# Unit 2 of a two-layer transformer kernel gets its Strassen projection, and attention's products move into the weights' slots

## The chip, the cores and the metric

The kernel runs on one core of one Trainium2 chip. A core has a matrix engine (TensorE, called PE in the profile, with its weight loads in a row of their own, PEld), a vector engine (VectorE, DVE), a scalar engine with table functions (ScalarE, ACT), a general engine (GpSimd, POOL) and a queue engine (SyncE, SP) that issues nearly all DMA transfers here. They run side by side and wait for each other by semaphores. SBUF is the memory on the chip in which all tiles lie; PSUM is the small memory of 8 banks into which TensorE writes. The metric is the device time of one execution, in microseconds; the time given for a kernel is the median of several runs.

## The reference: what is computed

The input is one sequence of 2048 tokens with 1024 channels in bf16. Two layers follow, and both use the same weights. Each layer is attention on the normalised input, added to the input, and then a feed-forward part on the normalised result, added again:

```python
x = x + _A_ref(_layernorm(x, axis=-1), A_wqkv, A_wo)
x = x + _B_ref(_layernorm(x, axis=-1), B_w1, B_b1, B_w2, B_b2)
```

`_A_ref` projects to q, k and v (1024 to 3 x 1024, 32 heads of 32 channels). A token attends to 8 tokens: itself and those 2, 4, ... 14 places before it. It takes the products of q with the 8 keys, a softmax over these 8 (places before the start are masked), and the weighted sum of the 8 values, and projects with `wo`. `_B_ref` is `h = x @ w1 + b1` (3584 wide), `relu(h)` squared, and `h @ w2 + b2`.

## The kernel before

**Units.** As the steps of the window are two tokens wide, even and odd tokens never meet in attention. The kernel takes the even tokens first and then the odd ones, so that a window is 8 neighbours in a row. A block is 512 such tokens (`BLK`), a layer has four blocks, and the two layers make 8 units, numbered 0 to 7. The units are staged so that the projections and the attention of unit u+1 stand beside the feed-forward part of unit u.

**Stages of one unit.** `SA` loads the tokens and normalises them (ScalarE) and transposes the result into `xnA`, with channels on the partitions. `SQ` or `SQ7` projects q, k and v. `S2` does attention, nearly all of it on VectorE, in two halves of 256 tokens: `prod` multiplies q with the eight shifted keys (tiles `P`) and adds pairs of them, TensorE sums over the channels of a head (`lg`), ScalarE takes the exponential, `norm` divides (`pb`), and `av` multiplies with the shifted values (tiles `pr`, 128 x 2 x 8 x 256, two channel groups in one tile) and adds the eight up into `o`. `SW` projects `o` with `wo` (PSUM tiles `py`), adds the residual (`xm`), normalises again and gives `xnB`. `SF1` computes the hidden layer into `r2`, and `SF2` multiplies it with `w2` and adds the residual (`xo`).

**Plain and Strassen forms.** A product of matrices cut into 2 x 2 blocks takes 8 block products, or 7 by Strassen's scheme in Winograd's form, at the price of sums and differences of the blocks of both operands and of the results. The weights are the same in both layers and in all units, so their combinations are made once on VectorE (tiles `tv`) and stored to DRAM by DMA, and later units load them. Unit 0 has plain forms in the feed-forward part (`SF1_plain`, `SF2_plain`), and while the weights are there it makes the combinations of `w1` (`keep_w1`, stored in `w1s`) and of `w2` (`keep_w2`, stored in `tw`). The units after it use seven products.

For q, k and v the constant `KEEPQ` says in which unit the combinations are made. Before, it is 2: units 0, 1 and 2 project plainly with `SQ` (line 729: 8 matmuls of 512 columns for each of 24 chunks of 128 channels), and `keep_wq` (line 771) makes the 24 combinations during unit 2's projection, each followed by a store to `wqsk` or `wqsqv`. From unit 3 on `SQ7` does it (line 851). It combines the blocks of the input on VectorE (`TA`, line 550: eight instructions). There are two steps for each of q, k, v, and a step takes 7 products of 8 matmuls of 256 columns in three PSUM banks X, Y, Z. Three times in a step the partial sum in X is copied out (`u`, line 837, ScalarE, or 838, VectorE), three times VectorE adds such a copy to another bank (line 842), and one result is copied out alone (829 or 830). That is 7 evictions where the plain form has 4 (lines 741 and 743) for the same outputs.

**Slots.** Each tile belongs to a class of slots of one size and takes a slot until its last reader is done. `8K` (9 slots of 8192 bytes a partition) holds the weight tiles `w`, the transposed inputs, `TA`, `T`, `o` and `s1`. `8P` (2 slots) holds nothing but `pr`. `2K` (8 slots) holds the combinations `tv` until their store has landed, the token tiles `xt` and `xn`, and the hidden layer's partial sums `rr`. Tags have caps besides: at most 6 `w`, 4 `tv`, 2 `pr`.

**The order of the work.** All operations are recorded first. Then the function `schedule` of class `Plan` orders them by a list scheduler that has a cost for each operation, a model of the DMA queue and the slots, and for every operation a priority and an engine pick (evictions and a few others can go to ScalarE or VectorE). The priorities and picks come from a packed table, `STARTS`, one entry for each operation. The order so found is what each engine gets; an engine executes its queue in that order and waits where an operand or a slot isn't free.

```python
def schedule(self):
    raw = zlib.decompress(base64.b85decode(STARTS))
    n = len(raw) // 3
    assert n == len(self.ops)
    for i, o in enumerate(self.ops):
        o.num, o.prio, o.pick = i, raw[i] + 256 * raw[n + i], raw[2 * n + i]
```

Of the kernel before, what the change touches and what calls it, by code (L numbers as in the profile page):

```python
# [12 lines left out]
F16 = mybir.dt.float16  # L13
# [4 lines left out]
H = 32  # L18
# [16 lines left out]
F_SW, F_H, F_QS, F_AV, F_ORD = 0, 1, 0, 1, 0  # L35
# [12 lines left out]
def _win_ap(a2d, col0, n, nw=W, wstep=-1):  # L48
# [5 lines left out]
    "c-rlG1zgu#(l>vlL%O?50qGP35fJG=DM(2w0us^)(p}PxlyrB8bR!4|2#O*GHY)0S&QI^|z5CqHvv=Qj_uczEpZ)&N%$b=pGiPT0iDH!Fo{3+f{Gji$$;4;YeQ@%F{GDS8ag(i6+Xu%uq%<%2^kJYK"  # L54
    "=8~Tr_7<&J`#0^CG59=K*qD`>Qs7QHPrwmw)KNfOt@hD`&R_mx0TwBjSi1c<XGEXSn*6lzT#etlhB2R*Zz6drW>{94260^polEEJ-Li|Sa>5Ts^?DZQ@LAq(pegyjKRc;Li#l@ud`xO(%R}^VO2O5D"
    "SQ2~wJdDWL0|{{!0!k-Y4t@6!JlEaY3t4a4*p5ze%6UE)k0aOD8#2h_h}mYeBX_)?f6{k8^HG8cw;^MbVLdv)rJ3I`x6CMaok_Qg)xIorYHd-}J)iXsDVKkeQpvvF3+>ZIZw=0tr+udJ{a}=L<PITE"
    "bk29R%FILWH5ajS7@yJ#Wrm3~yip(8v{KG{Jr#6rj8r82)`ebE2*3N*o@2OzR-{_kyY2DWP=m|2+k-p3HYL2L?|TMOq)6I(6n{N#dyD3V5m}#8@Ekgor-?w|>6Mij!OwiyVjOz8Q@U>|QhmAA9%z*Y"
    "ILvWkUSK@`kmS3dVc3_}-bIlHnoB%Z$98b}-%Pz^Y<+SMTc>H?CErr$1<6tdpXKUsS6j;#sas)UAGcjuwr6y>>%9eudy(%=Le5nOROd`|>@_~>IF!@XdH0?mqoXAxZC~c%{IS=PBpMoinMTDkyQ42d"
    "2IxI(CQ6x<1K&GiJXR^IKX-eL>WG9)mq#OExzvkV<*%~7FYCw{u|{}LJ5p-KN{uOG4S!F#D2F+I$Nd?@cAdwJFNRT?<vjnu3{U356Nk4O5=jP|RR>~1jjzwo5&N(D#QQkP_mZc7I^Fh~6Rqy!n$P~J"
    "_!jrxz+st_fZ2xE*T-zP*6z+w-O$xFxi^2U;HWUGj(;URwmwHiz_*2tCzWfO0Z!S`9b-)>Eu(V2@7$I8p-KH;`03PG#E$z{>kC%%Eg6K>KRo1@v>$K2DQR~<c>t46ZN)w<?D&O9{g4}OMHd{>&GKHc"  # L60
    "9FvoB7>J-)7O*0irZTv>@GRQ6bA{db>lp!`aq-ttSayxnL@(Q2jXJ`1kJwmFm*7be%Bp#XH5V@w-s{~jnj_rK7ok}@ryBo+{L--&3H(00YHZ>7@vd}-eP-K|Jy}(%_8!VJ(c=edJAEXPwxiYs{k*i|"
    "Lw59m<es#u@!eD^>OK+n%eWu8L~_nD3Xl6SiLmZ@9Cg+lk-V01Wj<ba(l8ufx^iugPTkir1K;Zfm&!4oOeV|6;j_GMYnr+>B=l2vwd@+qTY_9_Ur}akGlYK8N%jj%%x>Jc`!T6q-cN6#ui}Hv@keEk"
    "xy*TajrN<Z@KrDq+SVMM291kEx1}9@8!cMSzvL$O?ON~*pX(jB()XUCzdj#VeCX59VO`j&Wt+^MvnG0KCbYX)rR<Y>s_b*LEl1zZ0lrfP`zu}QNjz$u@B=Ny=0Pcuj6TX;jvj*ejh2)p*NrOn?q@v3"
    "SBjeUPe*yNJeCN|(rBj%wQZFO{95{C4qqpmQ$Ul)mT1*XFS_}2hBb!rod{ymMOKlMm7*~&od%uU?_(L3gC_WMA2AtWDHQD;M%-m4dir(@hgiv*B#bokYO|k^HIu{Yd(S?!=c6W!h4b=n*xGlMmcMVO"
    "Q3&|l#o;p@>MJA7N;hJCE8~Posa&!+cQ2|@tCc}LV+13MG|jB+9@cY)!qS%lCLzpq2ihsvUA`-HD(MwXhh8^kqayA-Il$4s>?Uw7nAy<#-N*5x`O7<I9`8&wLZ;Y^GfO#5xgARiX4TdmFkX8ROr5kS"
    "eL_KaPp_v^%ApolG&EKyC+t1P<%(rq3z43+2UM|>WY(=!+Tn+~0(?ixx4ujG)-Mp^>BnvbwHleP6k$c*+&6MN;aN>2-DoN9v0=6od5Etk+pqH^?XzL=ns=Q5-Aw=C5{bQ#Lm9@UPI8Sfx@(V|zu>SR"
    "kgbbm&hu9=R%3g}M?SnzoLqW{L&`vIvX9H$OzJ>XsLuMhQnOe1ol*etmwS%=gdKiIB7)T>QeSeIHGQv^_2{Vz5dMT~5$`3rj-i%vY%ldi5RF5HZ^>cUtk9VW<5#^4M7Gpx{twg(G27qlG0y8>>f*UE"
    "xgl1&S<XdX@z_`;4p;YR`FrkM8-WP(=7c525F=*3CP(6L-#t&(iiSR%-ZaK~E3%4fuKTtjigbgl_2Ihd2%ZJDQTP=ZQ7@(o#Z6zrmv^5KDoHp8#aLBlo^F-;(80e=-{P{=Lmc}#DtvHiUwZkdtnf4L"
    "kZY;BiCaS~=C!X47P`}HYBT*uC9mAmecne;QGsjm@q}s16Lxj;IK?OzoD)TPocE7*>YeA)dS<;7RD&hPq~V_{W<EjljP|sv`{(S6Q;~ufHT)g;T<bolaGXy*s+vJ0;PINrG}M75p_2$*^IYzzCu_;s"
    "*eA^7mt8P|776*S&&IiqcNpXkRX!rdF&zu<Ss}w!xb*HEUC5K=D^zAV4=PyeDFqVYJKjirQ%NK><3Q4;nF_lp>cu?WwY>evhvHXb2ixpOrCg7lwanNS>go7g9>1xhaH*s9m26QL(JtHGg3?Yeg^B$8"  # L70
    "R7a(xvDjM=IGuXlC`Qs&4xCdq(CYfA8Qw?Z@>HSTlJtc;Rp>x*ZQbdCRqws5Dl}bxg(GG3mSDJG#QH9?{GnDVtxy|AEc!?zA>HG7#%d4Qp38y<!jTV|iuqF&ymLvf%-Spo`p4a!B2+VCK9l{?zN-6)"
    "cXpI=-pc})w)c1Lq2!LIq)$_G30xmM;MP8njMY1;G>KKX#^Gie>NBxUR{YqENRg`u_sggb+Fz?tx6^N4bH*uv*L9GA^IO5>C(g3SFW0Lp6m&1406T8qyN4qf{%VVC<$kbXa@FoV`@rHz%%FioNs|mZ"
    "17iXX$4TtBlAnSVQ?!!V2{(NDzZVZ2+3CPae`x0wX;!c$MJn}<U(SwqSdZc=lT{Tt(*a2msc63b)(B^{nRWfm=g+1j;^&mzH>dgOY!s4JjlC=n>kjxfQe{?2yt&>+^?&>>*fnH|E<J@W&119|JQ?gP"
    "tLcvt(w7WeI-1C!I7_OJ<FzjlzrbnRhS7!6Jz^2;TBoF4pJLB%y-3u!bB0uvR@<;1LnSq;AE)Du|CUugp>6E)4hMf6=ePAl(b^5JfQowYruJ|ylxpi^cawysZXx#$C6~U9L22qO$2!TB$GEBzyTlPG"
    "a?&>Jq-w4F+mo60d78;%L}ydK$n#U2cO>tld2Ym{obFUjr#m_9?NZC}#!o5hQsueS(SYDHdmnL3QudVm7Os?Rh`W?~PAOFNQn9RmIH8PzgP%TYWxY0CNlDmJNJ40Rb=t<iWCwTHNw=1U*oD#XUW?Fj"
    "p2Zwr#=cAyJ8hk)`-Etz!O&I4P`ZBpn=8Vfl(Hywv&Jc_vb(c(xN@rB4a-cjYo;DlGjm<@*Pdb2Oex{=i{9r7xIwP}#m|Z~cRuE^MA@$LosSQ6R&itv!XkZM6k`RWt93%EzD<61PvCWbN-?>~@x?0)"
    "*TuG^{`1rQiwTQ%Ix%Y5<%{?PTb9d>gyJJ25)@>f&lLn(m;<&9`sCueF{y6Y*R0woe3e!Wp$ORTpruaT<w?$dv4gryuX3yKs#jn4x1xZm?ya3(ULT9T!9Hrb`<(u1CzrD8Ke*&x?|eq7d?EV7p0gfK"
    "EzLv_$EsM6zje)NvWf>hAKYWGM863rem;9YvFG;ur4*N=nK+sxZ&-utc3;nv%d?rgckmmPJBSrOW_M33xKb$*fgfA5h?)Dg)+u+H*fQhBgYf!ij~T@e3GApvFE5yO`aNom#Z{oL>Be|T{07h5x=A#7"
    "#j^ckz11K=K3(x+j=JF;we7Qc-@wm`WU1_gH+?K+i(Dl3vhGP^l+PV0)a9?+<?V{^-`X)$w2)BiJ>`Tu;FU$5K9gXY{gO^O;WdAN3(c@TI|I7XCI>TFxI2oJ+kWuUz*ltaFq3D=#<&}skGJh}Zv4v+"
    "H5G5ZJK@xDobpOn$?ox+8pQ{mN*al!`?x*R8#cvR`_*QdR=k{k6(2eagq`gLS9EfHzCU5BO|eS4u>1T>&{|Qn+ly^V>FI9`SljgPsO+C>%FTC>%yX7#7y6#s{kn6uY>g{#Zza0_1KY-k=v6!e^YSzk"  # L80
    "iOn~WgqrKCURE}Y*fM#<u@6U@4?{ZG9(6uRm=(No(x&Yxd10HP^sWM1yovD#f7Sb5n8ls%HNv>|E;w`eep1wqn#wL}&n$VZP@g@EXFeKt)+|rh&yhT$ckWRm#ck*Q4efrv*U}1<CWpe;B5zNyprf;E"
    "r-fP0++M(><a%qK_(9a4_r}M1qtCHRwQhqdddk&WpOtxy<gdPDSxsEq=jln%!!~f!Ex>1W#SVFqV=GCabfZR;ewzAg{nS^d?CL!6PtT4HzDw%E8s)LS^@VNkT*niWWQq$}n07m;f=>;Ye2<dn>#n8T"
    "+*nh)QTfQt`^z$M@mi3kJ7>3MSS{B@2BR6A(hbAm#mL3DM;?L1sLPoT?d!ir%?s$9XH8i^*_;YyT=qDXLnIyT7fLOVT=q)EeTeJ=uf?jou<7%Y4vr7drP$#c4bPZZy&4iDde*7rLt6!V**=9mZJ^Ld"
    "xb<GfYnH>F&v(pTtDc$x{hGIe&8+PCBiZ|S)Fri*k7bJ<sqED3DpbGJWiDP9!>6#|(-aT1^L{0G`9|sy=V2y~=mP28UGJEdAa#WX;<Wz4%G%9OBi2uCyE!t|aX$*Z@u<H)q|A8Lx4WCtwnT+2;Mq{%"
    "`%Y}LnX_p`hG}dGPvx6P4ey36r7!EAW?!d@=-oe9l5{3KBUaw={bU<)L@#~Z5Sy_ddhCdGrdn*?Rbmy#x>A07lX&-iSr+5HJQjnvN8DG?$y|QhlWYz(x$jl;NTt7tX@(uq$*Fm8d+jBLpW47nk}nsr"
    "`V8Y1=K{ND1ic;E=Y=rjBXA~pug`q>9(iXgm{0cO@o*Zoqjn8x1k1E_VVI33Rj&+7*S|>$*d{-m*~tI+Mr4-HsxdW&sKj!#kySfw36ntWHvXHI1;xlwT!s7E$sZghIImO^1$Jx84eV~6Po8Iq98nb|"
    "Z_Q|EQ$3W~NXEJ@u~*8z<jIHEM-<WeO~61V-{`i4j6<pXRM;yU#<`rAheYA)`*Yr9A`Tw6jr(MnbdpmB4zKlWbm575UMu`aykm)?*;nNgajg3;-z{sOmprz13#}Be%c|@iOko|f)`7;ACpC5~ytC7H"
    "hTS0*%Sa;qxlQ2)#fQOHPIuD}&+qVF^tYtDko93q*}v_(Y{y&q?t`q=7Zk%7d~R=qLmfV;CQkJ|=Xy8lR-3!Zh;~_CX0ez)K&c1U5xlfiy!l*`!z|<REWVOY-q0r+t@0RZG)dnl>Y4}hN>?lG%hHa^"
    "gk4+vde$>MT_CXk3yGHFpyzelIy}5?9&rl}o}R!L^vdofiznQC+@)p<Lq4xD7!csu%?$ETtJPQYAG_ILdn<AC>)Q2{kj4|HZvDmG#{25N@7OUgPyh%&f-u030AOJJI6)2(965UQ2o}~6ENo0nKv+jH"
# [262 lines left out]
class _Kernel:  # L352
# [522 lines left out]
    def S2(self, u, depths):  # L875
# [73 lines left out]

        def av(hb):  # L950
            pb = pbs[hb]
            if F_AV:
                for c in range(0, NCH, 2):
                    pr = Buf("8P", "pr", [128, 2, W, HB], F16)

# [471 lines left out]
```

## Time and profile before

| what | value |
|---|---|
| median of 5 runs | 1176.36 us (1174.65 to 1179.24) |
| the profiled execution | 1176.36 us, span 1174.6 us |
| mean granted clock of TensorE | 0.998 |
| busy: PE, PEld, DVE, ACT | 1154.3, 740.9, 1073.5, 659.3 us |
| DMA | 346.53 MB, mean 295 GB/s |

The span is the time between the first and the last record of the execution; the execution's own time has some 2 us around it. Busy times are of instructions; matmuls are pipelined, so that the busy time of PE is not the time that its streams need. In rows of instructions the first number is the start in us from the span's start, the second the time; "x16" is a number of instructions that follow each other; the brackets say how long the engine was idle before and what ended that. In rows of windows each engine has its busy time and, in brackets, its instructions, and the last three numbers are the granted clock, the DMA engines' busy share and GB/s.

### The profile page before, as it was taken

To read this page: it belongs to the slowest core of one execution; us is meant where nothing else is said; L and a number is where in the kernel's file an instruction comes from. 1 tells how busy PE (TensorE), PEld (TensorE's weight loads), DVE (VectorE), ACT (ScalarE), POOL (GpSimd) and SP (SyncE) were. 2 spreads that over 40 slices of the span, in tenths; PEclk is the share of its full clock that TensorE was granted. 3 is DMA by queue.
4 is the path that set the end of the run, shared out by engine and by line. 5 is a ranking of instruction groups with operands and counts; after the bars stand their busy time and mean duration, and the time that the engine had idled before them with its cause. 6 is when DMAs were issued, how large, how long until landed. Compare 5 with 4: busy or idle time off the path is not lost.

```text
span 1174.6 us, 19519 instructions
## 1 busy us (share of the span) xinstructions
PE 1154.3 (98%) x7607; PEld 740.9 (63%) x7607; DVE 1073.5 (91%) x1524; ACT 659.3 (56%) x1283; POOL 3.0 (0%) x10
## 2 busy tenths in 40 slices
PE   7999999999899999999999999999999999999998
PEld 4444444446755778467874678656885678844863
DVE  5899969999899999988999999998999999996872
ACT  6436981179741699217990479704995156915530
POOL 1000000000000000000000000000000000000000
PEclk9999999999999999999999999999999999999999
DMA  9526998889899799989999799988998888787774
GB/s 330 172 108 210 283 342 288 316 276 288 298 344 337 247 350 292 345 307 282 354 310 360 281 300 320 333 320 278 349 334 337 318 271 300 278 338 281 300 264 161
DMA packets 131325, 346.53 MB, mean 295 GB/s; under 512 B 63329, under 2 KB 71521, under 8 KB 109985
## 3 DMA queue, kind: packets, MB, share of 16 engines
q1 hardware_dynamic: 131008, 345.02, 85.8%
q8 instruction: 59, 0.97, 0.3%
q0 software_dynamic: 224, 0.28, 0.1%
q14 instruction: 34, 0.27, 0.1%
HBM read 302.26 MB, written 29.36 MB: 282 GB/s over the span
## 4 chain that ended last, share of the span: by engine, by line
PE 56%; DVE 5%; DMA 2%; ACT 1%; issue 0%; SPq 0%; DVEq 0%
PE X L1208 12%; PE X L1146 10%; PE X L851 6%; PE Z L1208 6%; PE py L1024 6%; PE Z L1146 5%; PE Z L851 3%; PE Y L1208 3%; PE Y L1146 2%; PE Y L851 2%; DVE P L904 1%; DVE P L896 1%; PE lg L911 1%; DMA w<-in_A_wqr_dram 1%; DVE rr L1118 1%; DMA xnA<-xn 1%
## 5 line engine op out<-in xcount | busy, mean ns | idle before, releaser
L1146 PEld LDWEIGHTS <-w 128*128 128x128 f16 (+1 forms) x2544 | 249.2, 98 | 44.5 <-issue 7.3
L1208 PEld LDWEIGHTS <-r 128*128 128x128 f16 x1176 | 114.9, 98 | 134.2 <-DMA w<-in_B_w_dram 1.4
L851 PEld LDWEIGHTS <-w 128*128 128x128 f16 (+1 forms) x1680 | 164.2, 98 | 30.6 <-issue 1.7
L1208 PE MATMUL X<-w,r 128*128 128x512 f16 (+1 forms) x784 | 179.5, 379 | 0.0
L837 ACT CAST u<-X 128x512 f16<-128x512 f32 x81 | 46.7, 582 | 212.9 <-PE X L851 212.6
L896 DVE TENSOR_TENSOR P<-q,k 128x2048 f16<-128x2048 f16 x128 | 153.6, 1221 | 1.1 <-ACT q L829 0.7
L957 DVE TENSOR_TENSOR pr<-pb,v 128x2048 f16<-128x2048 f16 x128 | 152.4, 1221 | 0.1
L1146 PE MATMUL X<-T,w 128*128 128x256 f16 x1072 | 133.0, 275 | 0.2 <-DVE u L1115 0.2
L729 PE MATMUL pq<-xnA,w 128*128 128x512 f16 x552 | 123.2, 379 | 0.0
L960 DVE TENSOR_TENSOR pr<-pr 128x1024 f16<-128x1024 f16 (+1 forms) x128 | 119.7, 947 | 0.0
L904 DVE TENSOR_TENSOR P<-P,P 128x2048 f16<-128x2048 f16 x96 | 116.8, 1216 | 0.3
L1024 PE MATMUL py<-w,o 128*128 128x512 bf16 x512 | 115.7, 379 | 0.0
L729 PEld LDWEIGHTS <-w 128*128 128x128 bf16 x552 | 53.9, 98 | 64.1
L851 PE MATMUL X<-TA,w 128*128 128x256 f16 x720 | 89.4, 273 | 0.0
L1114 ACT CAST u<-X 128x512 f16<-128x512 f32 x133 | 74.7, 582 | 21.9 <-PE X L1146 19.4
L1024 PEld LDWEIGHTS <-o 128*128 128x128 bf16 x512 | 50.0, 98 | 55.6
L1135 ACT ACTIVATE r<-rr 128x1024 f16<-128x1024 f16 (+1 forms) x75 | 73.6, 1000 | 7.0 <-DVE rr L1169 5.1
L589 ACT ACTIVATE xn<-xm 128x1024 f16<-128x1024 f32 x32 | 33.8, 1055 | 71.7 <-DVE xm L1028 70.2
L1118 DVE TENSOR_TENSOR rr<-u,Z 128x512 f16<-128x512 f16 x98 | 65.7, 679 | 1.1 <-PE Z L1146 0.4
L1028 DVE TENSOR_TENSOR xm<-py,xt 128x512 f32<-128x512 f32 x64 | 43.0, 683 | 14.2 <-PE py L1024 14.1
L1127 ACT ACTIVATE rr<-rr,b1T 128x256 f16<-128x256 f16 (+1 forms) x85 | 45.8, 564 | 13.3 <-DVE rr L1118 13.2
L922 ACT ACTIVATE e<-lg 128x512 bf16<-128x512 f32 x64 | 35.7, 599 | 28.4 <-PE lg L911 28.2
(143 smaller groups left out, 1658.7 us busy)
## 6 DMA issues: line engine op xcount, KB each, us to landing
w<-tw SPq DMA_DIRECT2D x56, 896.0 KB, 7.3
w<-w1s SPq DMA_DIRECT2D x45, 1024.0 KB, 7.7
w<-in_B_w_dram SPq DMA_DIRECT2D x42, 896.0 KB, 6.6
w<-in_B_w1r_dram SPq DMA_DIRECT2D x33, 1024.0 KB, 7.6
w<-in_A_wqr_dram SPq DMA_DIRECT2D x20, 1024.0 KB, 6.3
w<-wqsqv SPq DMA_DIRECT2D x20, 1024.0 KB, 6.9
w<-in_A_wqkv_dram SPq DMA_DIRECT2D x16, 1024.0 KB, 7.5
w<-in_A_wo_dram SPq DMA_DIRECT2D x16, 1024.0 KB, 7.2
```

The costliest lines, as they stand in the source:

```text
L729: nc.tensor.matmul(pq[:], wv(w, c0, kd), xnT[:, :, kd, :], start=(kd == 0), stop=(kd == KD - 1))
L851: nc.tensor.matmul(bank[:, a, :], w[:, wi, k, a * 128:(a + 1) * 128], rhs(k), start=(start and k == 0 and a == 0), stop=(k == 3), skip_gro ...
L896: nc.vector.tensor_tensor(cur[:], q[:, c, None, hb * HB:(hb + 1) * HB].to_broadcast([128, W, HB]), _win_ap(k[:, c, :], HALO + hb * HB, HB) ...
L904: nc.vector.tensor_tensor(other[:], other[:], cur[:], ALU.add)
L957: nc.vector.tensor_tensor(pr[:, i], pb[:], _win_ap(v[:, c + i, :], HALO + hb * HB, HB), ALU.mult)
L960: nc.vector.tensor_tensor(pr[:, :, 0:n], pr[:, :, 0:n], pr[:, :, n:2 * n], ALU.add)
L1024: nc.tensor.matmul(py[:], o[:, c, tl * 128:(tl + 1) * 128], wos[c // 4][:].rearrange("p (a b) n -> p a (b n)", a=4)[:, c % 4, sl], start=( ...
L1114: p.add("ACT", act(512), lambda: nc.scalar.copy(us[i][:], X[:]), [(X, 0)], [(us[i], 0)], UCOPY, name="u", alt=("DVE", dve(512, False), lam ...
L1118: p.add("DVE", dve(512, False), lambda: nc.vector.tensor_tensor(r[:, :, m, :], us[i][:], bank[:], ALU.add), [(us[i], 0), (bank, 0)], [(r, ...
L1135: p.add("ACT", act(len(ms) * 512), lambda: nc.scalar.activation(out=o(), in_=i(), func=ACTF.Square), [(r, (a, m)) for a in range(2) for m ...
L1146: nc.tensor.matmul(bank[:, a, :], w[:, wi, k, a * 128:(a + 1) * 128], rhs(k), start=(start and k == 0 and a == 0), stop=(k == 3), skip_gro ...
L1208: nc.tensor.matmul(banks[q][:], left(jj, q), w[:, j, :], start=(start and jj == 0), stop=(jj == h - 1), skip_group_check=True)
```

## The change

1. `KEEPQ` goes from 2 to 1. Unit 1 is now the unit in whose projection `keep_wq` makes the combinations and stores them, and unit 2 projects with `SQ7`.
2. The class `8P` is gone; `8K` grows from 9 to 11 slots of the same size, and `pr` takes its slots there. The cap of `w` goes from 6 to 7. The total of bytes is the same.
3. `STARTS` is replaced whole: every operation has a new priority, and the picks of engines are new too.
4. The old form of `av` with one channel group in a tile is taken out. It was not used (`F_AV` was 1). A flag `F_AVM` for a form with one wide multiplication is added, and is 0.

```diff
-F_SW, F_H, F_QS, F_AV, F_ORD = 0, 1, 0, 1, 0
+F_SW, F_H, F_QS, F_AVM, F_ORD = 0, 1, 0, 0, 0
...
 STARTS = (
...
-        self.KEEPQ = 2
+        self.KEEPQ = 1
...
-        sizes = [("8Q", 3, 8304), ("8K", 9, 8192), ("4K", 9 if F_AV else 12, 4096), ("8P", 2 if F_AV else 0, 8192), ("r2", 1, KF * BLK * 2), ("2K", 8, 2048), ("1K", 9, 1024),
+        sizes = [("8Q", 3, 8304), ("8K", 11, 8192), ("4K", 9, 4096), ("r2", 1, KF * BLK * 2), ("2K", 8, 2048), ("1K", 9, 1024),
...
-        p.caps.update(pk=2, lg=4, w=6, xt=3, P0=4, P1=4, pr=2, pb=2, dn=1, e=1, xm=6, xnA=1, TA=1, xnB=1, xn=2, xo=2, q=1, k=1, v=1, o=1, r2=1, s1=1, tv=4, T=1, wl=2)
+        p.caps.update(pk=2, lg=4, w=7, xt=3, P0=4, P1=4, pr=2, pb=2, dn=1, e=1, xm=6, xnA=1, TA=1, xnB=1, xn=2, xo=2, q=1, k=1, v=1, o=1, r2=1, s1=1, tv=4, T=1, wl=2)
...
             for c in range(0, NCH, 2):
-                    pr = Buf("8P", "pr", [128, 2, W, HB], F16)
+                pr = Buf("8K", "pr", [128, 2, W, HB], F16)
```

In the changed kernel the lines below `av` stand 15 lines earlier than before, and those in `av` one or two.

## The prediction

> **What bounds the kernel now.** I read the page's totals first, then the forms of the matmuls, then the timeline of TensorE for every place where it waits, then VectorE's windows at those places. The totals and the groups that the change touches:
>
> ```profile
> span 1174.6 us, 19519 instructions
> PE 1154.3 (98%) x7607; PEld 740.9 (63%) x7607; DVE 1073.5 (91%) x1524; ACT 659.3 (56%) x1283; POOL 3.0 (0%) x10
> ...
> L957 DVE TENSOR_TENSOR pr<-pb,v 128x2048 f16<-128x2048 f16 x128 | 152.4, 1221 | 0.1
> ```
>
> PE's 98% is a modelled figure, so I check it by streams. In the timeline 32 full-width matmuls (512 columns) go from 99.99 to 106.89 us, 0.2156 us each; 16 half-width ones (256 columns) go in 1.75 us, 0.1094 each. The run has about 3007 of the first and 4504 of the second: 648 + 493, with the transposes some 1147 of the 1174.6 us. What is left is the first 15 us, the last 3, and a handful of waits. So PE is the bound nearly everywhere, and a shorter stream of matmuls shows in the time wherever the others keep up. VectorE is the one that may not: between 40 and 1040 us its windows leave it idle 46 us (5%).
>
> Two waits matter here. The first, in the timelines of DVE and PE:
>
> ```profile
> 307.38 0.19 DVE L932 TENSOR_TENSOR e<-e,mask 128x56 bf16<-128x56 bf16 x1
> 311.66 0.69 DVE L1118 TENSOR_TENSOR rr<-u,Y 128x512 f16<-128x512 f16 x1 [4.09 <-DMA wqsqv<-tv]
> ...
> 307.19 1.91 PE L1146 MATMUL X<-T,w 128*128 128x256 f16 x16
> 312.40 1.03 PE L1146 MATMUL Z<-T,w 128*128 128x256 f16 x8 [3.30 <-DVE rr L1118]
> 313.27 3.51 PE L1146 MATMUL X<-T,w 128*128 128x256 f16 x16
> 316.57 1.15 PE L1146 MATMUL Z<-T,w 128*128 128x256 f16 x8
> ```
>
> `rr` and `tv` share the 2K slots. The last store of a weight combination (`wqsqv<-tv`) has not left its slot, VectorE stands 4.09 us for it, PE 3.30. Then 16 matmuls take 3.30 us (313.27 to 316.57) in place of 1.75: the clock is granted at half (the mean in the window of 276 to 345 us is 0.98). The place costs 3.30 + 1.55 = 4.85 us.
>
> The second is the passage of unit 0 from the output projection to the hidden layer, where nothing is lost now:
>
> ```profile
> 112.52 1.89 PE L1024 MATMUL py<-w,o 128*128 128x512 bf16 x8
> 114.25 0.61 PE L657 MATMUL pt<-ident,xn 128*128 128x128 f16 x8
> 114.69 3.62 PE L729 MATMUL pq<-xnA,w 128*128 128x512 f16 x16
> 118.15 0.61 PE L657 MATMUL pt<-ident,xn 128*128 128x128 f16 x8
> 118.59 3.62 PE L729 MATMUL pq<-xnA,w 128*128 128x512 f16 x16
> 122.41 0.62 PE L657 MATMUL pt<-ident,xn 128*128 128x128 f16 x8 [0.20 <-DVE xnB L660]
> 122.86 1.91 PE L1058 MATMUL ph<-xnB,w 128*128 128x256 f16 x16
> 124.97 15.27 PE L1054 MATMUL ph<-xnB,w 128*128 128x512 f16 x70 [0.20 <-DVE xnB L660]
> ...
> 80.00:120.00 40.00, 40.00 (x205) 18.85 (x204) 40.00 (x52) 22.61 (x44) 0.00 (x0) 1.00 0.51 179
> ```
>
> From the end of the last `py` (114.25) to the first full-width `ph` (124.97) the residual, two normalisations on ScalarE, transposes and copies take 10.7 us. PE has 10.0 us of other work to put there: three transposes, 32 projections of unit 1, 16 half matmuls. The window 80 to 120 has VectorE at 40.00 of 40: nothing more fits into it.
>
> **The change part by part.** *Matmuls.* Unit 2's 24 chunks of 8 full-width matmuls go: 192 x 0.2156 = 41.4 us. Six steps of 7 products of 8 half-width matmuls come: 336 x 0.1094 = 36.75 us. On the path, as PE is the bound there: **-4.65 us**. The instruction order of the changed kernel has these 144 extra matmuls, so the edit does what it says. Weight loads rise by 144; at 98 ns each they hide under 109 ns, as in the L851 stream that keeps 1.75 us per 16.
>
> *The store that held rr.* The 24 combinations of the weights and their 24 stores move from unit 2's projection (217 to 300 us) to unit 1's. In the changed order 16 are taken before the products of unit 0's second half block and the last 8 at least 85 us of matmuls before the first `rr`. The stores cannot be what `rr` waits for any more: **-4.85 us**. Behind it the same VectorE queue has the work of 424 us, where PE waited 2.07 and 0.50 us for `v` and `T`; that stays.
>
> *What the 16 combinations do to unit 0.* Each takes 0.60 us from start to start (102.60, 103.20): 9.6 us put into VectorE's queue ahead of unit 0's last products, in a stretch that has 4.5 us idle from 40 to 80 us and none from 80 to 120. Five casts (0.6 each) go to ScalarE, so the last `o` comes later and the planner fills PE with unit 1's projections first: in the changed order six of the eight `v` chunks stand ahead of the last four `py` groups, where four did before. Behind the last `py` are left three transposes, 16 projections and 16 half matmuls: 1.3 + 3.45 + 1.75 = 6.5 us. Against the 10.7 us of the chain, PE waits 4.2 us; VectorE's queue there (residual, copy, tree, three P, two tv, b2d, copy, tree, about 9.3 us to the last copy, against 8.8 now) says the same or 0.5 more. After 3.30 us of waiting the clock fell by half above, after 2.07 (424 us) it did not: 4.2 us brings 1.55 more. Less the 0.4 that is waited there now: **+5.35 us**. Ends: 0 if VectorE runs ahead, +10 if it waits for `tv` stores besides (rows of 4.2 and 3.7 us of such waits stand in the list of waits).
>
> [...]
>
> *Attention's products.* `pr` leaves its own two slots for the 8K pool, which grows from 9 to 11 with up to 7 weight tiles. Before, no `pr` waits for PE or a DMA (0.1 us idle before 128 of them). In the changed order about 25 of the first products name PE or a DMA among their waits, and 20 weight loads wait for VectorE (7 before). Behind a waiting `pr` stand the tree adds, the evictions and the residuals; behind a waiting load, all of SP's queue. The nearest row is the 4.09 us slot wait: one such event that reaches PE costs 4.85. I take **0**, as of the slot waits of DVE in the list (4.2, 4.1, 3.7) only one reached PE, and keep 0 to two events (9.7) for the range. The two weight tiles of unit 1's `v` also keep their slots some 60 us longer, until the last combination is made, so unit 0's hidden layer has five where it had six; a late tile there costs what `w1r` did at 424 us (2.3), inside that range. The seventh weight tile may end waits for loads (1.4 at L1208, 3.6 at L1146): down to -3.
>
> *Evictions.* Unit 2 gets 8 combinations of the input (0.34 us each by start to start) and 18 more evictions, on VectorE (0.60). The picks of engine changed too: by the counts in the order VectorE gains some 2 us over the run and ScalarE 14 (56% busy). Cover: PE's stream; if it is gone, 2 us. Taken as **0**. *DMA:* unit 2 loads 11.0 MB for 6.3 and no longer stores 6.3 there; the 16 early stores (4.2 MB) fall where 169 to 179 GB/s move of the 350 reached later. On SP's queue the first seven stand ahead of the second tile of `wo` and wait there for VectorE; the order puts that tile's first reader some 18 us later, and a `wo` tile lands in 7.2 us (page, part 6). POOL's queue is not passed. **0**. *The other handovers* (424, 700 to 708 us, some 5 us of waits): order redrawn, same kind; 0, ends -4 and +4.
>
> [...]
>
> Sum: -4.65 - 4.85 + 5.35 = -4.15 us. The profiled execution took 1176.36 us in all (span 1174.6), which is also the median of the five: 1172.2.
>
> **The rivals.**
> - *The passage of unit 0 costs more.* VectorE also waits for the stores of `tv` (16 more of them in that stage, through four buffers), one wait of 4.2 us on top: 1176.4, no change. For it: 40.00 of 40 in the window. Against: the DMA queue is half empty there.
> - *The passage costs nothing.* VectorE runs ahead of the written order, ScalarE's normalisations start early: 1176.36 - 9.5 = 1166.9. Against: the chain of 10.7 us is a measured one.
> - *Slower: products wait for weight slots.* Place: the first `pr` of each half block from unit 1 on. Price 4.85 us per event that reaches PE. One gives 1177; it decides against the change from two on: 1181.9. For it: VectorE has 5% idle, and 25 waits are new. Against: those slots come from weights that PE has consumed by the written order.
>
> **How the numbers follow.** The sum as written, 1168 to 1175 with the handovers' ends: 0.55. No cost at the passage: 0.10. Passage dearer or one slot event: 0.17. Two events or more: 0.18. What measurement of this kernel can tell from no change is 0.2%, 2.35 us: faster is under 1174.0, slower over 1178.7. Of the first case about 0.05 lies above 1174.0; so faster 0.60, same 0.21, slower 0.19. The range leaves out half of the cheap case and the upper half of the dear one: 1167 to 1181.
>
> **What would show it.** Right: no wait of VectorE for `wqsqv<-tv` before `rr`; the stretch of unit 2's projections some 4.7 us shorter; a wait of PE of 3 to 6 us before the first full-width `ph`, near 124 us, with a stretch at half clock behind it; 144 more matmuls; PE's total of streams 1142. Wrong: PE waits that VectorE's `pr` stands behind, more waits at the passages into the hidden layer of units 2 to 6, or a new store in front of `rr`.

## The result and the profile after

The changed kernel takes 1173.77 us (median of 30 runs, 1172.01 to 1175.31), the kernel before 1176.42 us (50 runs). The ratio is 0.9977, interval 0.9971 to 0.9983, so the change gains 2.0 to 3.4 us. The forecast was 1172.2, with a range of 1167 to 1181. The profiled execution of the changed kernel took 1172.72 us, 1.05 less than its median; between the two profiled executions lie 3.64 us.

The page's totals and the group of attention's products (line, instruction, tiles, count; busy time and mean ns of one; idle time ahead of them and what ended most of it):

```profile
span 1171.0 us, 19838 instructions
...
PE 1149.1 (98%) x7751; PEld 755.0 (64%) x7751; DVE 1078.9 (92%) x1528; ACT 675.0 (58%) x1305; POOL 3.0 (0%) x10
...
L956 DVE TENSOR_TENSOR pr<-pb,v 128x2048 f16<-128x2048 f16 x128 | 152.9, 1221 | 1.8 <-PE Z L1193 0.8
```

PE has 144 matmuls more (7607 to 7751) and 5.2 us less busy time. The 128 products waited 1.8 us in all, so sharing their slots with the weights cost nothing that can be seen.

To see where the time went I took, for each pair of neighbouring matmuls, the distance of their starts less the stream of the first (0.2156 us for 512 columns, 0.1094 for 256, 0.0563 for 128). What is left is waiting, or the clock at half:

| stretch, us | before: wait + half clock | after: wait + half clock | difference |
|---|---|---|---|
| streams of all matmuls | 1146.24 | 1141.60 | -4.64 |
| 0 to 40 | 2.68 + 2.49 | 2.76 + 2.66 | +0.25 |
| 120 to 140, passage of unit 0 | 0.74 + 0 | 5.04 + 1.43 | +5.73 |
| 280 to 320, first `rr` | 3.99 + 1.66 | 1.46 + 0 | -4.19 |
| 320 to 340 | 0 | 0.55 | +0.55 |
| 400 to 440 | 2.86 | 1.90 | -0.96 |
| 480 to 560 | 1.62 | 0 | -1.62 |
| 560 to 600 | 0.22 | 1.73 | +1.51 |
| 690 to 800 | 3.74 | 3.29 | -0.45 |
| ahead of the first, behind the last start | 8.10 | 8.33 | +0.23 |

They add up to -3.59 of the 3.64 us. Three rows make it: the streams, the stall that went, the stall that came.

The stall that came, in the timelines of PE and DVE (start, duration, idle time before and what ended it), and the window around it (granted clock is the third number from the end):

```profile
111.04 7.07 PE L1009 MATMUL py<-w,o 128*128 128x512 bf16 x32
117.95 0.61 PE L657 MATMUL pt<-ident,xn 128*128 128x128 f16 x8
118.40 3.62 PE L729 MATMUL pq<-xnA,w 128*128 128x512 f16 x16
121.85 0.61 PE L657 MATMUL pt<-ident,xn 128*128 128x128 f16 x8
122.30 1.91 PE L1043 MATMUL ph<-xnB,w 128*128 128x256 f16 x16
125.38 0.62 PE L657 MATMUL pt<-ident,xn 128*128 128x128 f16 x8 [1.17 <-ACT xn L567]
129.40 6.89 PE L1039 MATMUL ph<-xnB,w 128*128 128x512 f16 x24 [3.41 <-DVE xnB L660]
...
124.66 2.36 DVE L896 TENSOR_TENSOR P<-q,k 128x2048 f16<-128x2048 f16 x2
126.94 0.68 DVE L660 COPY xnB<-pt 128x1024 f16<-128x1024 f16 x1
127.54 1.21 DVE L904 TENSOR_TENSOR P<-P,P 128x2048 f16<-128x2048 f16 x1
128.67 0.68 DVE L660 COPY xnB<-pt 128x1024 f16<-128x1024 f16 x1
...
120.00:140.00 20.00, 15.42 (x84) 7.69 (x83) 20.00 (x24) 18.23 (x36) 0.00 (x0) 0.91 0.78 223
```

PE waits 1.17 and 3.41 us and then runs 24 matmuls in 6.89 us. The last transposes are ready at 126.00; the copy of them starts at 128.67, because VectorE first does two products `P`, the copy before and a sum. Its 20.00 of 20 are busy time, but not all of it is work that had to stand there.

At 300 us no wait for `wqsqv<-tv` is left: no row of VectorE's list of waits names it any more. The largest rows ahead of `rr` are now these (total us, times, longest):

```profile
DVE rr L1103 <- ACT u L1099: 4.9, 6, 1.4
DVE rr L1103 <- DMA xnA<-xn: 4.1, 2, 3.2
```

A smaller wait of the same kind came at 586, where `rr` waits for a slot that a transposing DMA holds:

```profile
587.80 0.69 DVE L1103 TENSOR_TENSOR rr<-u,Z 128x512 f16<-128x512 f16 x1 [3.21 <-DMA xnA<-xn]
...
588.54 1.03 PE L1131 MATMUL Z<-T,w 128*128 128x256 f16 x8 [1.65 <-DVE rr L1103]
```

### The profile page after: what moved, and what is told of

The parts are those of the page before. It is cut to its first block, busy times and chain, and to the rows that moved or that the text cites. A ratio compares the mean times of both kernels' runs of the same rounds, so it can differ in the third digit from the quotient of the medians.

```text
span 1171.0 us, 19838 instructions
## 1 busy us (share of the span) xinstructions
PE 1149.1 (98%) x7751; PEld 755.0 (64%) x7751; DVE 1078.9 (92%) x1528; ACT 675.0 (58%) x1305; POOL 3.0 (0%) x10
## 4 chain that ended last, share of the span: by engine, by line
PE 83%; DVE 8%; ACT 5%; DMA 3%; issue 1%; SPq 0%; DVEq 0%; ACTq 0%
PE X L1193 13%; PE X L1131 10%; PE X L851 9%; PE py L1009 8%; PE Z L1193 7%; PE pq L729 5%; PE Z L1131 5%; PE Z L851 5%; PE py L491 4%; PE ph L1039 4%; PE Y L1193 4%; PE Y L1131 3%; PE Y L851 2%; PE lg L911 2%; DVE P L896 2%; DVE P L904 2%
## 5 line engine op out<-in xcount | busy, mean ns | idle before, releaser
L1131 PEld LDWEIGHTS <-w 128*128 128x128 f16 (+1 forms) x2544 | 248.6, 98 | 42.3 <-issue 7.9
L851 PEld LDWEIGHTS <-w 128*128 128x128 f16 (+1 forms) x2016 | 197.2, 98 | 35.5
L837 ACT CAST u<-X 128x512 f16<-128x512 f32 x99 | 57.0, 581 | 212.2 <-PE X L851 208.0
L1131 PE MATMUL X<-T,w 128*128 128x256 f16 x1072 | 130.4, 273 | 1.0 <-DVE T L550 0.8
L851 PE MATMUL X<-TA,w 128*128 128x256 f16 x864 | 106.2, 273 | 0.0
L1099 ACT CAST u<-X 128x512 f16<-128x512 f32 x140 | 79.7, 581 | 27.2 <-PE X L1131 22.6
L1120 ACT ACTIVATE r<-rr 128x1024 f16<-128x1024 f16 (+1 forms) x79 | 79.5, 1013 | 5.1 <-DVE rr L1154 3.1
L729 PE MATMUL pq<-xnA,w 128*128 128x512 f16 x360 | 80.0, 379 | 0.0
L1103 DVE TENSOR_TENSOR rr<-u,Z 128x512 f16<-128x512 f16 x98 | 66.0, 681 | 10.7 <-ACT u L1099 4.9
L729 PEld LDWEIGHTS <-w 128*128 128x128 bf16 x360 | 35.2, 98 | 41.8
L1112 ACT ACTIVATE rr<-rr,b1T 128x256 f16<-128x256 f16 (+1 forms) x97 | 52.5, 563 | 12.1 <-DVE rr L1103 12.1
```

Of the source, the lines that this page charges most:

```text
L729: nc.tensor.matmul(pq[:], wv(w, c0, kd), xnT[:, :, kd, :], start=(kd == 0), stop=(kd == KD - 1))
L851: nc.tensor.matmul(bank[:, a, :], w[:, wi, k, a * 128:(a + 1) * 128], rhs(k), start=(start and k == 0 and a == 0), stop=(k == 3), skip_gro ...
L1099: p.add("ACT", act(512), lambda: nc.scalar.copy(us[i][:], X[:]), [(X, 0)], [(us[i], 0)], UCOPY, name="u", alt=("DVE", dve(512, False), lam ...
L1103: p.add("DVE", dve(512, False), lambda: nc.vector.tensor_tensor(r[:, :, m, :], us[i][:], bank[:], ALU.add), [(us[i], 0), (bank, 0)], [(r, ...
L1120: p.add("ACT", act(len(ms) * 512), lambda: nc.scalar.activation(out=o(), in_=i(), func=ACTF.Square), [(r, (a, m)) for a in range(2) for m ...
L1131: nc.tensor.matmul(bank[:, a, :], w[:, wi, k, a * 128:(a + 1) * 128], rhs(k), start=(start and k == 0 and a == 0), stop=(k == 3), skip_gro ...
```

## The experiments

Two theories were set against each other at each of three places: the stall that went, the stall that came, and what happens to time that is won there. In the edits below, a pair `(a, b)` puts operation `a` of the plan's list directly ahead of operation `b` in the finished order; everything else keeps its place.

### The stall at the first `rr`, alone

In the kernel before, one store of a combination of v's weights (919) is moved ahead of three weight loads in SP's queue (1117 is the first):

```diff
         order, self.timed = self.schedule()
+        for num, ahead_of in ((919, 1117),):
+            o = self.ops[num]
+            order.remove(o)
+            order.insert(order.index(self.ops[ahead_of]), o)
```

> The kernel before with one DMA moved: the last store of a combination of the weights of v stands ahead of three weight loads in the queue of SyncE (same order otherwise). Theory (the 4.09 us wait of VectorE for a slot of class 2K, held by that store, costs 3.30 us of TensorE and 1.55 us of half clock): both go, -4.85 us against the kernel before, 1171.5. Rival (another tile or the next store holds the slot as long, or the loads pushed back by 0.4 us come late in turn): less than half of that, above 1174.

Measured: 1171.89 us, ratio to before 0.9962 (0.9947 to 0.9977). The timelines of this run at the place:

```profile
309.85 0.19 DVE L936 TENSOR_TENSOR e<-e,mask 128x56 bf16<-128x56 bf16 x1
309.95 0.67 DVE L1122 TENSOR_TENSOR rr<-u,Y 128x512 f16<-128x512 f16 x1
...
309.66 1.91 PE L1150 MATMUL X<-T,w 128*128 128x256 f16 x16
311.41 1.04 PE L1150 MATMUL Z<-T,w 128*128 128x256 f16 x8
```

`rr` follows the mask at once, where it stood 4.09 us before, and PE doesn't wait. Between 280 and 320 us 5.65 us of waiting and half clock became 0.52. So the store's place in SP's queue, behind three weight loads, was the cause: the prediction had named the store, not the loads ahead of it. It also shows that this part of the gain did not need the change: one DMA moved in the kernel before gives at least as much as the whole change did.

### The slots, alone

The kernel before keeps its order, but its memory is divided as the change does it:

```diff
-        return pool.tile(b.shape, b.dt, name=b.tag, tag=b.cls, bufs=self.p.classes[b.cls][0])
+        tag, n = ("8K", 11) if b.cls in ("8K", "8P") else (b.cls, self.p.classes[b.cls][0])
+        return pool.tile(b.shape, b.dt, name=b.tag, tag=tag, bufs=n)
```

> The kernel before, its order of instructions untouched, but with the memory's slots as the change has them: pr and the 8K tiles draw on one pool of 11 slots in place of 2 and 9. Theory (sharing the slots costs nothing, as products never stand behind a slot that a weight holds): within 1 us of the kernel before, 1176. Rival (products wait for slots of weights, or weights for products): VectorE's idle time ahead of pr grows from 0.1 to several us, slower by 2 us or more. If the pool helps by itself, loads come earlier: faster by up to 3.

Measured: 1175.33 us, ratio 0.9986 (0.9974 to 0.9997). The group of the products in this run's page, and its timelines at the stall of `rr`:

```profile
L958 DVE TENSOR_TENSOR pr<-pb,v 128x2048 f16<-128x2048 f16 x128 | 153.2, 1230 | 0.1
```

```profile
311.84 0.69 DVE L1119 TENSOR_TENSOR rr<-u,Y 128x512 f16<-128x512 f16 x1 [3.80 <-DMA wqsqv<-tv]
...
312.58 1.03 PE L1147 MATMUL Z<-T,w 128*128 128x256 f16 x8 [3.01 <-DVE rr L1119]
313.45 1.91 PE L1147 MATMUL X<-T,w 128*128 128x256 f16 x16
```

The products wait 0.1 us as before: sharing the slots cost nothing here. The little that it is faster by, 0.3 to 3.1 us, I can't put down to the pool: in the profiled execution the 1.66 us at half clock behind the stall are missing (16 matmuls in 1.91, not 3.51), after a wait of 3.01 in place of 3.30. Why a wait that is nearly as long costs so differently is told in the last section. The changed order in the old slots was not tried.

### The stall at the passage: its price and its cause

First the half clock behind it. The changed kernel gets 14 idle matmuls where it waits, written into the bank that the first full-width `ph` (operation 393) then overwrites:

```diff
+        o = self.p.ops[393]
+        bank, real, g = next(b for b in o.bufs if b.cls == "ps"), o.fn, self.grp[:].rearrange("p h r -> p (h r)")
+        def fn():
+            for _ in range(14):
+                self.nc.tensor.matmul(bank.tile[:], g, g[:, None, :].to_broadcast([128, 4, 128]), start=True, stop=True)
+            real()
+        o.fn = fn
```

> The changed kernel with 14 idle matmuls of 512 columns (3.0 us) put into TensorE's queue where it waits before the first full-width ph of unit 0; their result is overwritten. Theory (the wait of 3.4 us makes the granted clock fall by half and this costs 1.4 us behind it): the ph starts at the same time, the stretch behind it has full clock, -1.4 us against the changed kernel, 1172.4. Rival (the clock falls for another reason, or the slow stretch costs nothing that lasts): no change, 1173.8; if the idle matmuls delay the ph, up to +1.

Measured: 1171.58 us, ratio 0.9957 (0.9942 to 0.9972), about 2 us below the changed kernel; the interval leaves 0 to 4. The timeline and the window:

```profile
125.43 3.19 PE L1331 MATMUL ph<-grp 128*128 128x512 f16 x14
129.00 11.17 PE L1039 MATMUL ph<-xnB,w 128*128 128x512 f16 x51 [0.39 <-DVE xnB L660]
```

```profile
120.00:140.00 20.00, 18.44 (x105) 9.37 (x104) 20.00 (x24) 19.32 (x39) 0.00 (x0) 1.00 0.78 214
```

`ph` starts as late as before (129.00 for 129.40), but 51 matmuls then take 11.17 us, 0.219 each, and the clock of the window is 1.00 for 0.91. The half clock was there because of the wait, and at this place filling the wait saves its 1.4 us. Not all of that arrives in the profiled execution: at 236 us it has a wait of 0.97 us for a load of `wo` that the changed kernel has not. That the median falls by 2 us all the same agrees with the clocks of the other executions: over the span 1.000 in all eight here, 0.997 in most of the changed kernel's.

Second, the order inside the passage. The last two copies of `xnB` (350, 361) go ahead of `tv`, `b2d` and `P` on VectorE, and the last normalisation (357, 358) ahead of a cast of v on ScalarE; 360 is the transposes, whose place on TensorE stays:

```diff
+        for num, ahead_of in ((350, 407), (360, 557), (361, 557), (357, 534), (358, 534)):
+            o = self.ops[num]
+            order.remove(o)
+            order.insert(order.index(self.ops[ahead_of]), o)
```

> The changed kernel with five operations moved at unit 0's passage from the output projection to the hidden layer: on VectorE the two last copies of xnB stand ahead of two combinations of w1, b2d and two products P, and on ScalarE one cast of v stands behind the normalisation. Nothing is left out. Theory (VectorE's queue, lengthened by the combinations of unit 1, sets the end of the passage): the wait of TensorE before the first full-width ph falls from 1.2 + 3.4 us to under 2 us, too short for the clock to drop, so the 1.4 us at half clock go too: -4.7 us against the changed kernel, 1169. Rival (the chain on ScalarE sets the end, VectorE's order is worth little): wait above 3.5 us, time within 1 us of 1173.8. Second rival (given back later, as VectorE has 5% idle and its products come 2 us later): passage short, but new waits further on, time within 1.5 us of 1173.8.

Measured: 1171.11 us, ratio 0.995 (0.9933 to 0.9968). The timelines and the window:

```profile
124.95 0.62 PE L661 MATMUL pt<-ident,xn 128*128 128x128 f16 x8 [1.17 <-ACT xn L571]
126.35 9.83 PE L1043 MATMUL ph<-xnB,w 128*128 128x512 f16 x37 [0.78 <-DVE xnB L664]
...
125.61 0.69 DVE L664 COPY xnB<-pt 128x1024 f16<-128x1024 f16 x1 [0.69 <-PE pt L661]
```

```profile
120.00:140.00 20.00, 18.05 (x96) 8.92 (x95) 19.27 (x22) 19.32 (x39) 0.00 (x0) 0.91 0.73 213
```

VectorE now waits for the transposes, not they for VectorE, and the wait of 3.41 is 0.78. That is what the expectation said; two things are not. The clock fell all the same (0.91): two waits of 1.17 and 0.78 us with eight short transposes between them were enough. And a new wait of 1.17 us came at 235 us. The profiled execution won 1.69 us of the 4.7 expected; the medians lie 2.66 us apart.

Third, are the early combinations in VectorE's queue what makes it late? The 16 of k and q are made cheaper, or taken to another engine:

```diff
-            p.add("DVE", dve(1024), lambda: nc.vector.tensor_tensor(t[:].rearrange("p k n -> p (k n)"), a(), b(), op), r, [(t, 0)], self.nxt(), name="tv")
+            few = nm != "v"
+            p.add("DVE", dve(1024), lambda: nc.vector.memset(t[:], 0.0) if few else nc.vector.tensor_tensor(t[:].rearrange("p k n -> p (k n)"), a(), b(), op), r, [(t, 0)], self.nxt(), name="tv")
```

and, in the other kernel,

```diff
-            p.add("DVE", dve(1024), lambda: nc.vector.tensor_tensor(t[:].rearrange("p k n -> p (k n)"), a(), b(), op), r, [(t, 0)], self.nxt(), name="tv")
+            eng = nc.gpsimd if nm != "v" else nc.vector
+            p.add("DVE", dve(1024), lambda: eng.tensor_tensor(t[:].rearrange("p k n -> p (k n)"), a(), b(), op), r, [(t, 0)], self.nxt(), name="tv")
```

> The changed kernel in which the 16 combinations of the weights of k and q (0.60 us each on VectorE) are replaced by clearing their tiles, an instruction that reads nothing and should take about half as long; the stores stay, the order stays. Left out: the values of these combinations, so units 2 to 7 project with zeros there; the amount of work elsewhere is the same. Theory (these instructions in VectorE's queue make the passage's wait): VectorE comes to the passage some 5 us earlier, the copies of xnB come right behind their transposes, TensorE's waits there fall from 4.9 to about 2.5 us in its starts, as in the run with the copies moved, and the time by 2 to 4 us against the changed kernel: 1170 to 1172. Rival (the combinations are hidden, the wait comes from ScalarE's chain and the written order of TensorE alone): waits stay at 4.9, time within 0.7 us of 1173.8.

Measured: 1173.58 us, ratio 0.9975 (0.9964 to 0.9985), the same as the changed kernel. VectorE's and TensorE's timelines:

```profile
83.61 1.22 DVE L937 TENSOR_TENSOR dn<-e 128x1024 f32<-128x1024 bf16 x1 [1.09 <-ACT e L923]
...
96.74 0.69 DVE L1014 TENSOR_TENSOR xm<-py,xt 128x512 f32<-128x512 f32 x1 [0.41 <-PE py L1010]
...
125.13 0.62 PE L657 MATMUL pt<-ident,xn 128*128 128x128 f16 x8 [1.17 <-ACT xn L567]
129.16 11.12 PE L1040 MATMUL ph<-xnB,w 128*128 128x512 f16 x40 [3.41 <-DVE xnB L660]
```

Clearing a tile takes 0.40 us from start to start, a combination 0.60, so 3.2 us left VectorE's queue. None of it reached the passage: VectorE waited for the exponential of the second half (from 0.43 in the changed kernel to 1.09 us) and for `py`, both of which TensorE releases, and TensorE comes to them when its own order says so: between 38 and 112 us it waits nowhere, here and in the changed kernel. So far as these 3.2 us of the 9.6 go, the rival holds: with copyfirst, the wait of 3.41 comes from the orders written for both engines.

> The changed kernel with the 16 combinations of the weights of k and q computed by GpSimd in place of VectorE, at the same places of the order; same results. Theory (the 9.6 us that these put into VectorE's queue make the passage's wait): VectorE comes to the passage's copies as soon as their data is there, the wait of TensorE falls from 4.6 to about 1.5 us, no half clock, -4.5 us against the changed kernel. Rival (TensorE's order, filled with projections ahead of the last py groups, makes the wait, whatever VectorE does): wait stays above 3.5 us, time within 1 us of 1173.8. If GpSimd is slow or disturbs VectorE, VectorE's mean times rise and weight tiles come later: slower than 1173.8.

Measured: 1199.64 us, ratio 1.0193 (1.0173 to 1.0213): the third case of the expectation, at a price that I had not thought of. The group on GpSimd, and the timelines of VectorE and TensorE:

```profile
L772 POOL TENSOR_TENSOR tv<-w 128x1024 f16<-128x1024 bf16 x8 | 27.6, 3474 | 37.2 <-DMA w<-in_A_wqkv_dram 37.2
```

```profile
63.55 9.17 DVE L957 TENSOR_TENSOR pr<-pb,v 128x2048 f16<-128x2048 f16 x3
...
92.91 3.24 PE L729 MATMUL pq<-xnA,w 128*128 128x512 f16 x8 [21.30 <-ACT k L741]
```

A combination of this group takes 3.5 us there in the mean, and while GpSimd works, three products of VectorE take 9.17 us, 3.1 each for 1.22. TensorE then waits 21.3 us for an eviction. This run says nothing about the passage. It shows how long the two engines take side by side, not what they contend for.

Fourth, could the combinations simply be made later? Seven of them are tied behind the last copy of `xnB` (361), and the planner orders anew:

```diff
+        last = self.ops[361]
+        for o in self.ops[302:315:2]:
+            o.prio += 2250
+            o.deps.append(last)
+            last.succ.append(o)
```

> The changed kernel with seven of the 16 early combinations tied by the planner behind the last copy of xnB of unit 0; the planner makes a new order from the same table. Theory (they can't simply be made later: until then they hold the slots of four weight tiles, which the loads of wo need): wo lands late, TensorE waits 5 us or more near 100 us, and the time is 15 us or more over the changed kernel, above 1188. Rival (the slots are not short): the wait at the passage falls and the time is below 1174.

Measured: 1200.59 us, ratio 1.0205 (1.0185 to 1.0224). SP's queue of this run, and TensorE's:

```profile
99.71 1.19 SPq L447 DMA_DIRECT2D w<-in_A_wqkv_dram  x2
```

```profile
96.93 3.62 PE L734 MATMUL pq<-xnA,w 128*128 128x512 f16 x16
106.70 1.03 PE L662 MATMUL pt<-ident,xn 128*128 128x128 f16 x8 [6.16 <-ACT xn L572]
```

It is not `wo` that pays, as I had written: the loads of v's weights are issued at 99.71, where the changed kernel issued them at 88.86, and TensorE, with no projection to put there, stands 6.16 us ahead of the next transposes. The profile has SP stand 28.9 us ahead of these loads for a `pq` matmul, the last reader of the weight tile whose slot they need. So the slots are short in this order. That the combinations, which hold weight tiles longer here, make them short is likely but not shown, as the whole order is new.

### What becomes of time that is won at the passage

Both remedies together: the copies moved as in copyfirst, and 5 idle matmuls ahead of the last transposes (360), 3 ahead of the first `ph`; `idle` does what the edit of warm does, for a given operation, number and bank. Then, in passage_wo, a step at the wait near 235 us, where combinations of `w2` (760) and the load of `wo` (863) are moved ahead:

```diff
+        idle(360, 5, lambda t: t[:].rearrange("p k n -> p (k n)").bitcast(F32))
+        idle(393, 3, lambda t: t[:])
...
-        for num, ahead_of in ((350, 407), (360, 557), (361, 557), (357, 534), (358, 534)):
+        for num, ahead_of in ((350, 407), (360, 557), (361, 557), (357, 534), (358, 534), (627, 774), (760, 627), (628, 630), (629, 630), (761, 775), (863, 775)):
```

> The changed kernel with the copies at unit 0's passage moved ahead as in the run copyfirst, and 5 + 3 idle matmuls of 512 columns (1.7 us) in TensorE's two waits that were left there (1.3 and 0.95 us). Theory (two short waits around eight transposes still let the clock fall, 1.48 us): full clock behind the passage, 1.4 us less than copyfirst's 1171.1: 1169.7. Rival (the time saved at the passage is eaten at unit 1's output projection, where the second tile of wo came 1.2 us late in copyfirst): time as copyfirst, the wait near 235 us grows to 2.5.

> As passage_both, and near 220 us three combinations of w2 stand ahead of a product pr on VectorE, and the second load of wo for unit 1 ahead of one store on SyncE. Theory (that load waits for VectorE's combinations, which hold its slot or stand in front of it in the queue): the wait of 1.2 to 2.5 us near 235 goes, 1 to 2 us less than passage_both: 1168.5. Rival (the load is bound by the DMA engines): same time as passage_both.

Measured: passage_both 1171.99 us, ratio 0.9959 (0.9944 to 0.9975); passage_wo 1172.47, ratio 0.9968 (0.9956 to 0.9981). The clock is full in both profiled executions, and the passage with its idle matmuls costs 3.06 us in place of 6.47 (1.72 of matmuls, 1.34 of the rest). But it didn't arrive: new waits stand at 173 and 235 us. In passage_wo they only changed places (3.14 us between 140 and 240, against 1.80), so that edit was no remedy.

To see who makes these waits, all combinations of `w1` and `w2` are cleared instead of computed, in passage_both:

```diff
-            p.add("DVE", dve(n * BLK), lambda: nc.vector.tensor_tensor(t[i][:, :n], a(), b(), ALU.subtract), r, [(t[i], 0)], 45.0, name="tv")
+            p.add("DVE", dve(n * BLK), lambda: nc.vector.memset(t[i][:, :n], 0.0), r, [(t[i], 0)], 45.0, name="tv")
...
-            p.add("DVE", dve(1024), lambda: nc.vector.tensor_tensor(t[:], a(), b(), op), r, [(t, 0)], self.nxt(), name="tv")
+            p.add("DVE", dve(1024), lambda: nc.vector.memset(t[:], 0.0), r, [(t, 0)], self.nxt(), name="tv")
```

> passage_both with all combinations of w1 and w2 replaced by clearing their tiles (0.40 from start to start on VectorE in place of 0.60): some 19 us less of VectorE's work between 44 and 240 us, stores and order as they are. Left out: the values of those combinations. Theory (the time won at the passage comes back at 173 and 235 us because VectorE has under 5% idle from 40 to 240 us and paces the loads there): the waits of 1.2 and 0.6 us go, 1.8 us less than passage_both, 1170. Rival (those waits are DMA transfers that take their time, whatever VectorE does): they stay, time as passage_both, 1172.

Measured: 1169.56 us, ratio 0.9941 (0.9929 to 0.9954). First passage_both's timeline of TensorE and its windows (the third busy time is VectorE's), then those of paced:

```profile
174.51 2.75 PE L495 MATMUL py<-w,r 128*128 128x512 bf16 x12 [1.02 <-DVE py L508]
...
236.48 2.75 PE L1013 MATMUL py<-w,o 128*128 128x512 bf16 x12 [0.39 <-DMA w<-in_A_wo_dram]
...
140.00:240.00 100.00, 98.60 (x513) 49.89 (x511) 96.12 (x136) 46.31 (x87) 0.00 (x0) 1.00 0.96 321
```

```profile
172.82 2.75 PE L495 MATMUL py<-w,r 128*128 128x512 bf16 x12
...
233.37 3.78 PE L1013 MATMUL py<-w,o 128*128 128x512 bf16 x16
...
140.00:240.00 100.00, 100.00 (x523) 51.06 (x522) 89.90 (x137) 46.49 (x87) 0.00 (x0) 1.00 0.97 325
```

With VectorE 6.2 us less busy in these 100 us both waits are gone, the one for the DMA of `wo` too, whose loads stand behind VectorE's combinations in SP's queue. So between 140 and 240 us VectorE paces the kernel as soon as TensorE comes earlier: of the 3.4 us won at the passage 1.6 were given back there.

Last, the order of TensorE at the passage itself: two projections of v (437, 509) behind the last `py`, and four combinations of `w1` (378 to 384; the stores follow) behind the copies of `xnB`:

```diff
-        for num, ahead_of in ((350, 407), (360, 557), (361, 557), (357, 534), (358, 534)):
+        for num, ahead_of in ((350, 407), (360, 557), (361, 557), (357, 534), (358, 534), (378, 407), (380, 557), (382, 557), (384, 557), (379, 412), (381, 412), (383, 412), (385, 412), (437, 533), (509, 533), (438, 534), (510, 534)):
```

> As copyfirst, and besides two of unit 1's projections of v (3.45 us of TensorE) stand behind the last four py groups of unit 0 in place of ahead of them, and four combinations of w1 on VectorE (2.4 us) behind the last copy of xnB in place of ahead of the last o; no idle matmuls. Theory (the wait at the passage is made by the last o, which VectorE reaches late, and by the projections that TensorE's order spends before it): the last py ends some 3 us earlier, the two projections fill the wait, waits at the passage under 1 us and no half clock: 3.7 us less there than copyfirst. Of that some 1.5 us may come back as waits between 140 and 240 us, as in passage_both: time 1168 to 1170. Rival (the last o is bound by what stands before it, so that TensorE now waits ahead of py instead): a wait of 3 us near 108 us, time as copyfirst, 1171.

Measured: 1174.49 us, ratio 0.9984 (0.9975 to 0.9994); a miss. The timelines of TensorE and ScalarE:

```profile
109.93 6.22 PE L1013 MATMUL py<-w,o 128*128 128x512 bf16 x28 [1.17 <-DVE o L966]
...
127.75 10.52 PE L1043 MATMUL ph<-xnB,w 128*128 128x512 f16 x48 [0.78 <-DVE xnB L664]
140.09 1.89 PE L1043 MATMUL ph<-xnB,w 128*128 128x512 f16 x8 [1.82 <-ACT r L1051]
143.88 7.07 PE L1043 MATMUL ph<-xnB,w 128*128 128x512 f16 x32 [1.90 <-ACT r L1051]
...
129.94 1.06 ACT L593 ACTIVATE xn<-xt 128x1024 f16<-128x1024 bf16 x1 [3.16 <-DVE tv L536]
```

The passage itself is short, at full clock. But the last `o` did not come earlier (TensorE now waits 1.17 us ahead of `py`): VectorE again stood for `py`, 1.39 us at 97.13. And the combinations that were moved hold 2K slots later, so ScalarE waits 3.16 us for a slot of `xn`, the ReLU behind it is late, and TensorE pays 3.7 us. The price is the one that the kernel before paid at 308 us, for the same class of slots.

## Why the prediction was right

*Matmuls, -4.65.* Measured -4.64 in streams, with 144 more matmuls. Nothing in it was off.

*The store that held rr, -4.85.* The stall is gone, and moved alone it gives 5.13 us at its place. The changed kernel has 1.46 us of other small waits in the same stretch, so that net -4.19 is left.

*The passage of unit 0, +5.35.* Measured +5.73: waits of 1.17 and 3.41 us for the 4.2 of the working, 1.43 us at half clock for 1.55. The size was right and the reason half right. That TensorE's filling was spent ahead of the last `py`, and that the chain behind it then had 6.5 us of cover, is what the timeline shows. That the combinations in VectorE's queue delay it on the chip is what early_half speaks against: the 3.2 us that it took out of 9.6 went into longer waits of VectorE for what TensorE releases. What is left is that they act through the written orders. Nor is the chain of 10.7 us a given: 2.6 us of the wait behind it were the order of VectorE's queue, which copyfirst changed. And the lengths from which the half clock was drawn (after 3.30 us yes, after 2.07 no) are no rule, as the last section shows.

*Attention's products, 0.* Right: 1.8 us of waiting in all, and nothing in the run with the slots alone. The rival of two or more slot events did not happen. *Evictions and DMA, 0.* No wait of TensorE over 0.5 us that names a DMA or an eviction of `SQ7` was added outside the handovers. *The other handovers, 0 with ends -4 and +4.* By the table -0.96, -1.62, +1.51, -0.45 and +0.55, together -0.97: their sum was small, though single ones reach 1.6 us.

The sum of -4.15 stands against -3.64 between the two profiled executions. Between the medians it is -2.65, as this profiled execution lies 1.05 us below the changed kernel's median. That rest is not in any step of the sum, and where it lies is open. The granted clocks point at windows at half: seven executions of the changed kernel, the profiled one among them, have 0.998 over the span and a median of 1172.60, while 23 have 0.997 and 1173.99. In early_half, whose waits at the passage are the same, the stretch at half is 6.83 us long in place of 3.41, and the passage costs 7.24 us in place of 6.47. The first 40 us, where the first loads land, vary too (5.17 us of waits and half clock in the kernel before, 7.61 in storefirst).

The time fell with TensorE's streams while VectorE's busy time rose by 5.4 us, so for the whole kernel the streams were the right measure. For the 100 us behind the passage it is VectorE that has to be relieved once TensorE comes earlier, as paced shows.

A better version: copyfirst, 1171.11 us, is faster than both kernels. Not tried: unit 2's Strassen projection with an order searched for it alone, and a table searched with the price of the half clock in it.

## What to carry to other kernels

Look at every stall that a change removes and ask for the cheapest edit that removes it alone: here one DMA moved ahead of three others (1171.89 us) gave at least what 144 matmuls, eleven slots and a new table gave together (1173.77). In a kernel with written orders, ask whether work taken off an engine arrives downstream: in early_half 3.2 us taken off VectorE went into its waits for TensorE, which was full, and the wait of 3.41 us at the passage stayed. Move the instruction that is waited for (copyfirst: 3.41 became 0.78 us), and then look further for the engine that paces there (passage_both: new waits at 173 and 235 us, some 50 and 110 us behind). When tiles of different lives share a class of slots, follow each moved tile's release, not only its start (o_early: 3.16 us for a slot of `xn`).

## What the runs showed of the hardware

*In these executions the clock fell by windows, not by waits.* In the profile's record of the granted clock every stretch at half behind a wait lasts 3.41 us or a multiple of it (3413 ns at 313.4 us before, 3413 ns at 129.2 us after, 6.83 us in early_half), and within one execution they all lie on one grid: before, the stretches at full clock on either side are 303.786 and 856.745 us, 89 and 251 times 3.4133; after, 119.466 and 1037.652 us, 35 and 304 times. I cut the profiled executions of 13 kernels, 4401 such windows at full clock that end before the last matmul, along this grid. All 11 windows in which TensorE streamed less than 34% of the time were followed by one at half; of the five with 37 to 42% one was; of the rest, none. Before, the window from 310.0 us (29%) was followed by half clock and the next emptiest, from 13.0 us (42%), was not; after, the one from 125.8 us (2%) was and the one from 586.6 us (47%) was not. So a wait of 2.59 us (gpsimd, 613 us) and two of 1.17 and 0.78 (copyfirst) cost some 1.6 us of half clock each, and one of 3.01 (shared_slots) none: by these counts it was the share of a window that the waits emptied, and so where the grid cut them, that decided.

*GpSimd beside VectorE (gpsimd).* The 16 combinations of 128x1024 take 3.47 (8 of them), 2.78 (4) and 2.72 us (4) on GpSimd in the mean, for 0.60 on VectorE from start to start. Between 63 and 92 us VectorE's 128x2048 products beside them take 3.1 us for 1.22; one at 49.31 us took 1.22, and there GpSimd's two combinations took 11.05 us together. These 16 instructions on GpSimd cost 26 us (1199.64 for 1173.77).
